# Centring two row pairs before PE turns them, with their layer-norm scale applied where values and key exponentials leave PSUM, and a new order of all steps

## The chip, the core and the metric

The kernel runs on one core of a Trainium2 chip. Five engines work beside each other, each with its own list of instructions: PE (matrix products and turns), ACT (activations, copies out of PSUM), DVE (vector work), POOL (elementwise work, memsets) and SP (which issues nearly all DMAs here). They meet through semaphores. The metric is the device time of one execution in microseconds. Before, it is 151.34 us (median of 3 runs, 151.34 to 151.38).

## What is computed

Rows x (2048 x 448) are layer-normalized to xn. The result is x plus a linear attention with a softmax feature map plus a dense layer with Mish, both on xn:

```python
xn = _layernorm(x, axis=-1)
return x + _A_ref(xn, A_wqkv, A_w_phi, A_wo) + _B_ref(xn, B_w1, B_b1, B_w2)
# _A_ref, 16 heads of 28:
pq = jnp.einsum("bhsd,hdf->bhsf", q, w_phi)
pk = jnp.einsum("bhsd,hdf->bhsf", k, w_phi)
phi_k = jnp.concatenate([_softmax(pk, axis=-1), _softmax(-pk, axis=-1)], axis=-1)
kv = jnp.einsum("bhsf,bhsd->bhfd", phi_k, v)
z  = jnp.einsum("bhsf->bhf", phi_k)
# phi_q likewise; num = phi_q kv, den = phi_q z + 1e-6, o = num / den, then o @ wo
# _B_ref: h = xn @ w1 + b1, act = Mish(h), act @ w2
```

The layer norm is (x - mean) / sqrt(var + 1e-5), without weights. So a row's scale, 1/sqrt(var + eps) (rstd), can be applied behind a product instead of ahead of it: (x - mean) W times rstd is xn W.

## The kernel before, in words

Tokens are handled as 16 tiles t of 128 rows, taken in 8 pairs u (tiles 2u and 2u+1). For each pair: statistics of both tiles (`ln_stats`: bn_stats and bn_aggr on DVE, or for one tile of the pair two passes with a sum on ACT), the scale (`ln_rstd` on ACT as Ln and Exp, or on POOL as a power), the normalized rows (`ln_pair` on DVE or POOL, three operations into one of four buffers xn), and the turn (`xT`: seven 128 x 128 blocks, by PE and copied out of PSUM into xnT, or as one DMA transpose from SP). A pair holds 7 blocks, since 448 = 3.5 x 128 and the two half blocks share one.

The turned rows feed the projections: `v_mm` (values), `k_mm` (keys, already through the feature map: the weights Wk and w_phi are multiplied once into Wpk, by `w_tr`, which turns Wk, and `w_mm`, which multiplies with the block-diagonal Wbd), `q_mm` (the same with Wpq) and `ffn1` (dense layer, W1). Such a projection holds two PSUM banks, one per tile, and is split into parts A, B (6 passes each) and H (2 passes); a pass is a matmul over 64 rows of the contraction, and two passes on the two halves of the array run side by side. All of it goes through the helper `run`, line 423. When the last part is done, ACT or DVE takes the banks out: keys and queries as Exp with both signs (L618 and L680), values as a copy (L510 or L512), the dense layer as Mish (L699). There are four pairs of banks, so at most four results are open.

Behind the keys, `k_norm` divides the exponentials by their sums (sums on DVE, the product on POOL, L630), `kv_mm` (L649) sums phi_k v over all rows, `kvz` turns that by a DMA, and `nd` (L722) gives numerators and denominators per tile; DVE divides, a DMA turns the result, `wo` (L845) and `ffn2` (L828) add up the output, DVE adds x (L793) and the rows are stored. The last tile is cut into 384 and 64 columns.

What sets the order is the string ORDER: it names every step, `run_order` calls them one after the other, and each call appends its instructions to the lists of the engines. Each engine works strictly in this order; semaphore waits come from the resources that a step reads and writes. A step's name carries kind, pair and engine: `xt2b` turns pair 2 by PE and copies it out on both ACT and DVE, `xt1m` turns pair 1 by DMA, `rs1a` is pair 1's scale on ACT, `wtk0b` and `wmk0b` are the turn and the product of the first half of Wk, `wmq0d` the query product with DVE copying out, `qd` the copy on DVE that doubles a part of WqT for that product, `lx1s` a load from SP (x2, x3, ... are row pairs; x4 and x6 load two pairs at once; `lkms` and `lvms` the main parts of Wk and Wv, `lkts` the last 64 rows of both, once per array half, called tails below; `lps` Wraw, that is w_phi; `l1ms`, `l1ts` the same of W1), `z12` twelve dummy matmuls of 512 columns on zeros (`warm`, L364), which keep PE working until the first data are there.

## Time and profile before

| what | value |
|---|---|
| time, median of 3 runs | 151.34 us |
| span of the profiled execution, first to last instruction | 148.7 us |
| that execution's own time around the span (151.34 - 148.7) | 2.6 us |
| ACT busy | 74.5 us (50%) |
| DVE busy | 102.4 us (69%) |
| POOL busy | 38.8 us (26%) |
| granted TensorE clock over the span | 1.000 |
| x loads of one pair, issue to landing | 3.0 us (4 loads of 224 KB) |

The page gives busy time per engine, a chain of work that ended last, and groups of instructions with their mean. The timeline gives rows in order of time: start, length, engine, line and operation, result and operands with shapes, count, and in brackets the idle time ahead of it with its releaser. A row with "x26" covers 26 instructions that follow one another. SPq rows are DMA issues; their landing is listed apart. Matmul lengths include the pipeline, so the pace is read from the starts or from a row's length over its count.

### The profile page before, as it was taken

The page shows a single profiled execution, that of the slowest core. Times are in us where ns is not written, and L with a number is a line of the kernel's source. Part 1 is how long each engine was busy: PE and PEld are TensorE (multiplying, and loading weights), DVE is VectorE, ACT ScalarE, POOL GpSimd, SP SyncE. Part 2 cuts the span into 40 slices and gives each one's busy share as a digit, 9 for nine tenths or more (in the row PEclk, how much of TensorE's full clock was granted, in tenths as well). Part 3 has the DMA queues.
Part 4 walks back from the last instruction along what each step waited for, and adds up shares of the span by engine and source line. Part 5 has one row for each costly group of instructions (what it writes and reads, how often), then busy time and mean ns, then how long its engine had stood idle before and what let it go on. Part 6 is the DMA issues. An engine that isn't in the chain of part 4 may idle for free.

```text
span 148.7 us, 3867 instructions
## 1 busy us (share of the span) xinstructions
PE 144.3 (97%) x1669; PEld 74.4 (50%) x1669; DVE 102.4 (69%) x229; ACT 74.5 (50%) x91; POOL 38.8 (26%) x53
## 2 busy tenths in 40 slices
PE   6999999999999999999999999999999999999993
PEld 2375555555544554444544445545555555555562
DVE  0599898996999940407697879539983999930072
ACT  3987999879999999657757762002000000000000
POOL 4423475079999993000000000000000000000000
PEclk9999999999999999999999999999999999999999
DMA  4998678799499159399856053120013040542005
GB/s 133 240 270 232 138 143 158 128 169 334 102 194 191 30 49 132 69 223 283 225 120 121 0 66 62 27 39 0 7 21 102 20 108 0 123 100 85 4 0 185
DMA packets 39964, 17.23 MB, mean 116 GB/s; under 512 B 33932, under 2 KB 39180, under 8 KB 39948
## 3 DMA queue, kind: packets, MB, share of 16 engines
q1 hardware_dynamic: 39776, 16.89, 53.4%
q8 instruction: 13, 0.21, 0.6%
q10 hardware_dynamic: 172, 0.10, 0.2%
q14 instruction: 3, 0.02, 0.0%
HBM read 7.02 MB, written 1.84 MB: 60 GB/s over the span
## 4 chain that ended last, share of the span: by engine, by line
PE 96%; DVE 1%; POOL 0%; issue 0%; POOLq 0%
PE PS L423 50%; PE PS L828 29%; PE PS L845 7%; PE PS L364 4%; PE PS L722 3%; PE PS L649 2%; PE PS L580 1%; DVE xn L497 1%; PE PS L505 1%; DVE x_all L793 0%; POOL v_all L339 0%; PE PS L556 0%; DVE x_all L814 0%; DVE b1T L512 0%; PE PS L693 0%
## 5 line engine op out<-in xcount | busy, mean ns | idle before, releaser
L423 PE MATMUL PS<-xnT,W 64*128 64x512 bf16 x392 | 44.8, 377 | 0.0
L828 PE MATMUL PS<-W,actT 128*128 128x448 bf16 (+1 forms) x224 | 42.9, 351 | 0.0
L699 ACT ACTIVATE actT<-PS,b1T 128x1024 bf16<-128x1024 f32 x28 | 29.8, 1112 | 22.1 <-PE PS L423 22.1
L828 PEld LDWEIGHTS PS<-W,actT 128*128 128x128 bf16 x224 | 21.5, 98 | 19.8 <-issue 0.3
L423 PEld LDWEIGHTS PS<-xnT,W 64*128 64x128 bf16 x392 | 18.0, 94 | 21.9 <-PE PS L423 1.9
L630 POOL TENSOR_TENSOR actT<-actT,rSk 128x896 bf16<-128x896 bf16 x16 | 26.6, 1699 | 5.1 <-DVE rSk L628 5.1
L793 DVE TENSOR_TENSOR x_all<-PS,x_all 128x448 bf16<-128x448 f32 (+1 forms) x16 | 9.2, 614 | 15.1 <-PE PS L845 10.5
L626 DVE TENSOR_REDUCE Sk<-actT 128x32 f32<-128x896 bf16 x16 | 16.6, 1037 | 1.1 <-ACT actT L618 1.1
L618 ACT ACTIVATE actT<-PS 128x896 bf16<-128x896 f32 x16 | 13.7, 920 | 1.8 <-PE PS L423 1.7
L423 PE MATMUL PS<-Wpk,xnT 64*128 64x448 bf16 x112 | 13.2, 349 | 0.0
L423 PE MATMUL PS<-Wkv,xnT 64*128 64x448 bf16 x112 | 12.9, 349 | 0.0
L423 PE MATMUL PS<-Wpq,xnT 64*128 64x448 bf16 x112 | 12.6, 349 | 0.0
L738 DVE COPY Sq<-PS 128x16 f32<-128x16 f32 x32 | 4.0, 167 | 12.0 <-PE PS L722 12.0
L462 DVE BATCH_NORM_STATS2 stats<-x_all 128x6 f32<-128x448 bf16 x14 | 8.4, 601 | 3.5 <-DMA x_all<-in_A_x_dram 3.5
L746 DVE TENSOR_TENSOR v_all<-v_all 128x464 f32<-128x464 f32 x16 | 10.3, 642 | 0.6
L742 DVE TENSOR_TENSOR v_all<-PS,Sq 128x464 f32<-128x464 f32 x16 | 10.3, 641 | 0.5
L749 DVE TENSOR_TENSOR xn<-v_all,rden 128x448 bf16<-128x448 f32 x16 | 10.0, 626 | 0.6
L744 DVE TENSOR_TENSOR v_all<-PS,Sq 128x464 f32<-128x464 f32 x16 | 10.1, 630 | 0.0
L680 ACT ACTIVATE actT<-PS 128x896 bf16<-128x896 f32 x10 | 8.6, 930 | 0.1
L423 PEld LDWEIGHTS PS<-Wpq,xnT 64*128 64x128 bf16 x112 | 5.4, 94 | 5.0 <-ACT actT L680 0.2
L423 PEld LDWEIGHTS PS<-Wkv,xnT 64*128 64x128 bf16 x112 | 5.4, 94 | 5.0 <-ACT actT L618 0.2
L423 PEld LDWEIGHTS PS<-Wpk,xnT 64*128 64x128 bf16 x112 | 5.4, 94 | 5.1 <-issue 0.2
(83 smaller groups left out, 119.3 us busy)
## 6 DMA issues: line engine op xcount, KB each, us to landing
W<-in_B_w_dram SPq DMA_DIRECT2D x1, 1568.0 KB, 9.3
...
W<-in_B_w_dram SPq DMA_DIRECT2D x1, 1344.0 KB, 6.5
...
```

Source lines behind the costliest of these rows:

```text
L423: ins = e.matmul(o, lhs(c, k), rhs(c, k), start=first and n == at[par][0], stop=last and n == at[par][-1])
L618: op("ACT", lambda e, s=s: e.activation(E_of(u)[:, s, :, :], two(b, D), ACT.Exp, scale=1.0 if s == 0 else -1.0), r=[pb(b), pb(b + 1)], w=[ ...
L626: op("DVE", lambda e: e.tensor_reduce(Sk[u][:, s, :], Eh(), AX.X, ALU.add), r=[("E", u, s)], w=[("Sk", u, s)], tag=f"Sk{u}.{s}")
L630: op("POOL", lambda e: e.tensor_tensor(Eh(), Eh(), ap_on(rSk[u][:, s, 0:1], [[1, 2 * H], [0, DH]]), ALU.mult), r=[("E", u, s), ("rSk", u, ...
L699: op("ACT", lambda e: e.activation(actT[:, fc, q * 1024:(q + 1) * 1024], bank(b, 2), ACT.Mish, bias=b1T[:, fc:fc + 1]), r=[("b1T",), pb(b) ...
L742: op("DVE", lambda e: e.tensor_tensor(tv(t1[i]), num(0), sx(1), ALU.mult), r=[pb(b), pb(b + 1), ("Sq", i, 1)], w=[("t1", i)], tag=f"ta{t}")
L744: op("DVE", lambda e: e.tensor_tensor(tv(t2), num(1), sx(0), ALU.mult), r=[pb(b), pb(b + 1), ("Sq", i, 0)], w=[("t2",)], tag=f"tb{t}")
L746: op("DVE", lambda e: e.tensor_tensor(t1[i], t1[i], t2, ALU.add), r=[("t1", i), ("t2",)], w=[("t1", i)], tag=f"tc{t}")
L749: op("DVE", lambda e: e.tensor_tensor(o_sb[(t // 2) % 2][:, t % 2, :].rearrange("p (h d) -> p h d", d=DH), t1[i][:, :, 0:DH], ap_on(rden[i ...
L793: op("DVE", lambda e: e.tensor_tensor(x_all[:, t, 0:n], bank(b)[:, 0:n], x_all[:, t, 0:n], ALU.add), r=[pb(b), ("x", t)], w=[("out", t)], ...
L828: ins = e.matmul(bank(b)[:, 0:width(t)], actT[:, fc, tok(t)], W2[:, fc, 0:width(t)], start=first and fc == 0, stop=last and fc == FC - 1)
L845: ins = e.matmul(bank(b)[:, 0:w], oT_of(u)[lo:hi, cc * P:(cc + 1) * P], Wo[lo:hi, cc, 0:w], start=first and n == at[par][0], stop=last and ...
```

## The change

Pairs 2 and 3 (CENT) are treated in two ways. For their values and keys the rows are only centred (`center`: x - mean, three operations on DVE), turned by PE (`xcT`) and copied into a free row of actT, not into xnT. The scale is applied at the exit: values leave PSUM tile by tile with scale rstd, and the exponentials of the keys as four activations of 448 columns with scale rstd or nrstd = -rstd (`neg_rstd`) in place of two of 896 with scale 1 or -1. For their queries and the dense layer, which need normalized rows in xnT, both pairs are normalized once more (`ln_pair` on POOL: xn3p, xn2p) and turned by DMA (xt3m, xt2m).

Statistics are now steps per tile (`st_dve`, `st_mean`, `st_var`), so that a mean can be had ahead of a variance. Both halves of Wk are turned into a pair of banks and copied out by ACT and DVE; of its last 64 rows only one copy is turned, and the copy out of PSUM doubles it. The tails of Wkv are loaded as keys and values together for one array half, values alone for the other. The dummy matmuls read a constant of ones that is there at the start, and there are eight. And ORDER is new throughout.

```diff
-pv table lx2s lba zero pm st2b lx3s lkms lps st3b lkts z12 pi b1 rs2p pw rs3a xn2d bd lx1s wtk0b lvms lx4s xn3d xt2b
-wtk1b wmk0b lqT2 xt3a v2Ha wmk1a v2Ba lqT0 st1 v3Ha lqT1 lqT3 rs1a v3Aa v2Aa st4 rs4p pk v3Ba k3H lx0s k3A qd xn1d
+lx3s lba pv lx2s pw sd6 table sm7 sm5 pi lkms lps z8 xc7 sv7 lt0s lvms lt1s pm xc6 bd lx1s sd4 lqT2 lx4s xc5 sv5 xc4
+b1 lqT1 ct3 wtk0b wtk1b ct2 rs2a sd3 sd2 sd9 wmk0a rs1a wmk1a rs3p nr2p xn3p lx6s xn1d sd8 sd11 v3Ha v2Hd v3Bd v2Ba
...
-                ins = e.matmul(bank(b)[:, :], ap_on(zeros[:, 0:1], [[0, P]]), ap_on(zeros[:, 0:1], [[0, TCW]]), start=True,
-                               stop=True)
+                ins = e.matmul(bank(b)[:, :], ap_on(ones, [[0, P]]), ap_on(ones, [[0, TCW]]), start=True, stop=True)
...
+    def load_kv_tail(eng, i):
+        (lo, hi), at = HALF[i], (0, D)[i]
+        dma(eng, lambda e: e.dma_start(Wkv[lo:hi, 3, at:2 * D], A_wqkv[384:448, D + at:3 * D]), w=[("Wt", i)],
+            tag=("ldWkv", "ldWvt")[i])
...
+    def center(t):
+        u = t // 2
+        for n, (lo, hi, at) in enumerate(parts_of_row(t)):
+            op("DVE", lambda e, lo=lo, hi=hi, at=at: e.tensor_scalar(
+                xn[u % NXN][:, at:at + hi - lo], x_all[:, t, lo:hi], mv[:, t, 0:1], None, op0=ALU.subtract),
+               r=[("x", t), ("mean", t)], w=[("xn", u % NXN, t % 2, n)], tag=f"xc{t}.{n}")
+
+    def neg_rstd(u, eng):
+        op(eng, lambda e: e.tensor_scalar(nrstd[:, 2 * u:2 * u + 2], rstd[:, 2 * u:2 * u + 2], -1.0, None, op0=ALU.mult),
+           r=[("rstd", u)], w=[("nrstd", u)], tag=f"nr{u}")
...
+    def xcT(u):
+        i = u % NXN
+        b = take2(False)
+        pe(lambda e: transpose7(e, b, xn[i], 3), [("xn", i, 0, 0), ("xn", i, 1, 0), ("xn", i, 1, 1), ("ident",)],
+           [pb(b), pb(b + 1)], f"xT{u}c")
+        for eng, lo, hi, bb, n in (("ACT", 0, 3, b, 0), ("DVE", 3, 7, b + 1, 1)):
+            at = (u % 2) * 7 * P
+            evac(eng, lambda lo=lo, hi=hi: actT[:, CROW, at + lo * P:at + hi * P],
+                 lambda lo=lo, hi=hi, bb=bb: bank16(bb)[:, 0:(hi - lo) * P], [pb(bb)], [("xcT", u, n)],
+                 f"xT{'hf'[n]}{u}c")
...
+    def scaled(eng, dst, src, t, r, w, tag):
+        if eng == "ACT":
+            op("ACT", lambda e: e.activation(dst(), src(), ACT.Copy, scale=rstd[:, t:t + 1]), r=r, w=w, tag=tag)
+        else:
+            op("DVE", lambda e: e.tensor_scalar(dst(), src(), rstd[:, t:t + 1], None, op0=ALU.mult), r=r, w=w, tag=tag)
...
     def k_mm(u, part):
         def then(b):
+            if u in CENT:
+                for s in range(2):
+                    for i in range(2):
+                        op("ACT", lambda e, s=s, i=i: e.activation(
+                            E_of(u)[:, s, i, :], bank(b + i)[:, 0:D], ACT.Exp,
+                            scale=(rstd, nrstd)[s][:, 2 * u + i:2 * u + i + 1]),
+                           r=[pb(b + i), ("rstd", u), ("nrstd", u)], w=[("E", u, s)] if i else [("Eh", u, s)],
+                           tag=f"exkc{u}.{s}{i}")
+                return
```

What the new order moves is shown at three places. The first is PE's start, from the dummies on. L364, L693, L556, L505, L580 and L423 are the dummies, the turn of the bias b1, the turns of Wk, the turns of rows, the products with Wbd and the projections' passes. Before:

```order
L364 MATMUL PS<-zeros 128x512 x12
L693 MATMUL PS<-ident,b_rows 128x14
L556 MATMUL PS<-ident,Wkv 112x128 x8
L505 MATMUL PS<-ident,xn 128x128 x7
L556 MATMUL PS<-ident,Wkv 112x128 x8
L580 MATMUL PS<-Wbd,Eq 128x112 x8
L505 MATMUL PS<-ident,xn 128x128 x7
L423 MATMUL PS<-Wkv,xnT 128x448 x2
L580 MATMUL PS<-Wbd,Eq 128x112 x8
L423 MATMUL PS<-Wkv,xnT 128x448 x26
L423 MATMUL PS<-Wpk,xnT 128x448 x8
L580 MATMUL PS<-Wbd,WqT 128x112 x16
```

The same place now (the lines are those of the changed kernel):

```order
L376 MATMUL PS<-const-bfloat16-1.0 128x512 x8
L759 MATMUL PS<-ident,b_rows 128x14
L529 MATMUL PS<-ident,xn 128x128 x7
L590 MATMUL PS<-ident,Wkv 112x128 x12
L590 MATMUL PS<-ident,Wkv 112x64 x4
L529 MATMUL PS<-ident,xn 128x128 x7
L614 MATMUL PS<-Wbd,Eq 128x112 x16
L434 MATMUL PS<-Wkv,actT 128x448 x28
L434 MATMUL PS<-Wpk,actT 128x448 x22
L614 MATMUL PS<-Wbd,WqT 128x112 x16
```

A turn of rows stands first now, both halves of Wk follow one another, the two products with Wbd too, and no value pass stands ahead of them; 22 key passes in place of 8 stand ahead of the query product.

The second place is ACT, from the scale of the first pairs to the first values. Before:

```order
L510 ACTIVATE Eq<-PS 112x512 [waits done_PE]
L510 ACTIVATE xnT<-PS 128x384 [waits done_PE]
L510 ACTIVATE Eq<-PS 112x512 [waits done_PE]
L510 ACTIVATE Wpk<-PS 128x448 [waits done_PE]
L510 ACTIVATE xnT<-PS 128x896 [waits done_PE]
L510 ACTIVATE Wpk<-PS 128x896 [waits done_PE,done_DVE]
L476 ACTIVATE lnv<-mv,eps_col 128x2 [waits done_DVE]
L478 ACTIVATE rstd<-lnv 128x2 [waits done_ACT]
L510 ACTIVATE v_all<-PS 128x32x28 [waits done_PE] x2
```

There now (Eq is the buffer that holds the turned Wk, lnv and rstd are the scale):

```order
L534 ACTIVATE actT<-PS 128x384 [waits done_PE]
L534 ACTIVATE Eq<-PS 112x512 [waits done_PE] x2
L534 ACTIVATE actT<-PS 128x384 [waits done_PE]
L487 ACTIVATE lnv<-mv,eps_col 128x2 [waits done_ACT]
L489 ACTIVATE rstd<-lnv 128x2 [waits done_ACT]
L534 ACTIVATE Wpk<-PS 128x896 [waits done_PE,done_DVE]
L487 ACTIVATE lnv<-mv,eps_col 128x2 [waits done_DVE]
L489 ACTIVATE rstd<-lnv 128x2 [waits done_ACT]
L534 ACTIVATE Wpk<-PS 128x896 [waits done_PE]
```

Pair 1's scale, which waits for DVE's statistics of pair 1, stood behind the second copy of Wpk; now it stands ahead of it.

The third place is SP's queue, from the last turns of WqT on. L517 (now L541) are the DMA turns of rows, L688 (L754) those of query exponentials, L278 (L285) the tails of W1. Before:

```order
L270 DMA x_all<-in_A_x_dram 128x896
L270 DMA x_all<-in_A_x_dram 128x1792
L517 DMA_TRANSPOSE xnT<-xn 128x7x128 [waits done_DVE]
L278 DMA W<-in_B_w_dram 64x1792 x2
L517 DMA_TRANSPOSE xnT<-xn 128x7x128 [waits done_DVE]
L517 DMA_TRANSPOSE xnT<-xn 128x7x128 [waits done_POOL]
L688 DMA_TRANSPOSE EqT<-Eq 128x8x128 [waits done_ACT]
```

There now:

```order
L541 DMA_TRANSPOSE xnT<-xn 128x7x128 [waits done_DVE]
L541 DMA_TRANSPOSE xnT<-xn 128x7x128 [waits done_POOL]
L277 DMA x_all<-in_A_x_dram 128x896
L285 DMA W<-in_B_w_dram 64x1792 x2
L541 DMA_TRANSPOSE xnT<-xn 128x7x128 [waits done_POOL]
L541 DMA_TRANSPOSE xnT<-xn 128x7x128 [waits done_DVE]
L280 DMA W<-in_B_w_dram 128x3x1792
L541 DMA_TRANSPOSE xnT<-xn 128x7x128 [waits done_POOL]
```

These are the turns of pairs 1 and 3, a load of x and the tails of W1, then pairs 4 and 6, W1's main part, and pair 5. Before, pairs 1, 4 and 5 were the first three turns by DMA, and W1's main part was loaded behind all of them. Further on, all query projections stand ahead of the dense layer's first passes, where before three of them stood among those, and the KV products, which were spread over three places, stand together ahead of the sixth group of the dense layer.

More of the change, by code (lines that the diff above doesn't have):

```diff
@@ L227, in _kernel, with xcT_of @@
     FE = FC - NU
+    CENT = (2, 3)
+    CROW = 3
+    def xcT_of(u, c):
+        return actT[:, CROW, (u % 2) * 7 * P + c * P:(u % 2) * 7 * P + (c + 1) * P]
     def E_of(u):
@@ L311, in table @@
            tag="table")
-    def p_zero():
-        op("POOL", lambda e: e.memset(zeros[:], 0.0), w=[("zeros",)], tag="zeros")
     def p_ident():
@@ L445, in step, with st_dve, st_mean, st_var @@
         return add
[L449 to L465 removed]
+    def st_dve(t):
+        op("DVE", lambda e: e.bn_stats(stats[:, t, :], x_all[:, t, :]), r=[("x", t)], w=[("st", t)], tag=f"bn{t}")
+        op("DVE", lambda e: e.bn_aggr(mv[:, t, :], stats[:, t, :]), r=[("st", t)], w=[("mv", t), ("mean", t)],
+           tag=f"ag{t}")
+    def st_mean(t):
+        i = t // 2 % 2
+        op("ACT", lambda e: e.activation(junk[i][:], x_all[:, t, :], ACT.Copy, scale=1.0 / D, accum_out=mv[:, t, 0:1]),
+           r=[("x", t), ("junk", i)], w=[("mean", t), ("junk", i)], tag=f"sm{t}")
+    def st_var(t):
+        i = t // 2 % 2
+        op("ACT", lambda e: e.mul(rmean[:, i:i + 1], mv[:, t, 0:1], D ** -0.5), r=[("mean", t)], w=[("rmean", i)],
+           tag=f"rm{t}")
+        op("ACT", lambda e: e.activation(junk[i][:], x_all[:, t, :], ACT.Square, bias=rmean[:, i:i + 1],
+                                         scale=-D ** -0.5, accum_out=mv[:, t, 1:2]),
+           r=[("x", t), ("rmean", i), ("junk", i)], w=[("mv", t), ("junk", i)], tag=f"sq{t}")
     def ln_rstd(u, eng):
@@ L620, in then @@
                    r=[pb(b), pb(b + 1)], w=[("E", u, s)], tag=f"exk{u}.{s}")
-        pair_part(f"k{u}", part, tok_works(u, Wp[1]), [("xnT", u), ("xnU", u)] + [("Wp", 1, h, c) for h in range(2) for c in range(2)], then)
+        pair_part(f"k{u}", part, works_of(u, Wp[1]), turned(u) + [("Wp", 1, h, c) for h in range(2) for c in range(2)], then)
     def k_norm(u, s):
@@ L701, in then @@
                r=[("b1T",), pb(b), pb(b + 1)],
-               w=[("act", fc, q)] + ([("E", fc - FE, s) for s in range(2)] if fc >= FE else
+               w=[("act", fc, q)] + [("xcT", u, n) for u in CENT for n in range(2) if fc == CROW] + ([("E", fc - FE, s) for s in range(2)] if fc >= FE else
                                      [x for i in range(3) if EQ_ROWS[i] == fc for x in (("Eq", i, 0), ("Eq", i, 1), ("Eqp", i))]), tag=f"mish{q}_{fc}")
@@ L867, in _kernel @@
     for u in range(NU):
-        add(f"st{u}", ln_stats, u)
-        add(f"st{u}b", ln_stats, u, True)
+        for t in (2 * u, 2 * u + 1):
+            add(f"sd{t}", st_dve, t)
+            add(f"sm{t}", st_mean, t)
+            add(f"sv{t}", st_var, t)
+            add(f"xc{t}", center, t)
+        for eng, c in (("DVE", "d"), ("POOL", "p")):
+            add(f"nr{u}{c}", neg_rstd, u, eng)
+        add(f"ct{u}", xcT, u)
         add(f"xt{u}b", xT, u, "both")
@@ L911, in _kernel @@
             add(f"l{n}m{c}", load_main, eng, "W" + n, t, A_wqkv[:, (i + 1) * D:(i + 2) * D])
-        add(f"lkt{c}", load_tail, eng, "Wkv", Wkv, A_wqkv[:, D:3 * D])
+        for i in range(2):
+            add(f"lt{i}{c}", load_kv_tail, eng, i)
         add(f"l1m{c}", load_main, eng, "W1", W1, B_w1)
@@ L921, in _kernel @@
     add("qd", double_qT)
-    for n, fn in (("pi", p_ident), ("pm", p_mask), ("pw", p_wbd), ("pv", p_ones), ("pk", p_kvt), ("pp", p_pads), ("zero", p_zero)):
+    for n, fn in (("pi", p_ident), ("pm", p_mask), ("pw", p_wbd), ("pv", p_ones), ("pk", p_kvt), ("pp", p_pads)):
         add(n, fn)
-    for n in (1, 2, 4, 8, 12):
+    for n in (6, 8, 10, 12):
         add(f"z{n}", warm, n)
```

109 lines of the change are left out of this document (55 added, 54 removed).

## Prediction

> **What bounds the kernel now.** I read the page's busy table first, then the chain of work that ended last, then the timeline of the first 16 us.
>
> ```profile
> PE 144.3 (97%) x1669; PEld 74.4 (50%) x1669; DVE 102.4 (69%) x229; ACT 74.5 (50%) x91; POOL 38.8 (26%) x53
> ```
>
> PE is busy almost all of the time. Busy is not the same as useful, so the chain in order of time (start, length, what) comes next.
>
> ```profile
> 1.39 5.30 PE PS L364 x12
> ...
> 10.72 3.32 PE PS L423 x34
> 14.04 0.89 PE PS L580 x16
> 14.94 36.24 PE PS L423 x370
> 51.18 0.88 PE PS L649 x96
> ...
> 59.45 7.90 PE PS L423 x72
> ...
> 143.25 2.42 PE PS L828 x14
> ```
>
> The first 5.30 us are twelve dummy matmuls. From 10.7 us on, PE runs one pass of the projections (L423, 448 columns, two half-arrays side by side) every 3.32/34 = 0.098 us, and 36.24/370 = 0.098 us over the next 36 us. It holds this pace without a gap, and only the last addition and store follow 145.7 us. So the kernel is "time at which PE becomes dense" plus a fixed amount of PE work plus a tail. A change can win only ahead of 10.7 us, and every wait of PE behind that point is lost in full.
>
> What holds PE back ahead of 10.7 us is in the timeline (start, length, engine, line, operation).
>
> ```profile
> 3.54 0.58 ACT L453 ACTIVATE junk<-x_all 128x448 bf16<-128x448 bf16 x1 [1.46 <-DMA x_all<-in_A_x_dram]
> 4.02 0.19 ACT L453 ACTIVATION_READ_ACCUMULATOR junk<-x_all 128x1 f32 x1
> ...
> 6.63 0.19 ACT L458 ACTIVATION_READ_ACCUMULATOR junk<-x_all,rmean 128x1 f32 x1
> ...
> 6.94 1.13 DVE L497 TENSOR_SCALAR xn<-x_all,mv,rstd 128x448 bf16<-128x448 bf16 x3
> 6.99 0.82 PE L556 MATMUL PS<-ident,Wkv 128*112 128x128 bf16 x8 [0.18 <-DMA Wkv<-in_A_wqkv_dram]
> 7.32 1.16 POOL L539 TENSOR_TENSOR Wbd<-Wraw,mask 112x224 bf16<-112x224 bf16 x2 [0.52 <-DMA Wraw<-in_A_w_phi_dram]
> 7.84 0.60 ACT L510 ACTIVATE Eq<-PS 112x512 bf16<-112x512 bf16 x1 [0.46 <-PE PS L556]
> 8.32 0.88 DVE L497 TENSOR_SCALAR xn<-x_all,mv,rstd 128x448 bf16<-128x448 bf16 x3
> 8.53 0.61 PE L556 MATMUL PS<-ident,Wkv 128*112 128x128 bf16 x8
> 8.73 0.49 ACT L510 ACTIVATE xnT<-PS 128x384 bf16<-128x384 bf16 x1 [0.29 <-PE PS L505]
> ...
> 9.86 0.36 PE L423 MATMUL PS<-Wkv,xnT 64*128 64x448 bf16 x2
> 10.65 2.63 PE L423 MATMUL PS<-Wkv,xnT 64*128 64x448 bf16 x26
> ```
>
> The row statistics (on ACT from 3.54 to 6.63 + 0.19 = 6.82), then the scales and the normalized rows (DVE, 6.94 and 8.32), run ahead of PE's turns of pairs 2 and 3. Two other chains run beside them and depend on no row of x: the key weights land at 6.99 and are turned and copied out; the feature matrix Wraw lands at 7.3 and POOL builds Wbd until 7.32 + 1.16 = 8.48. At 10.65 all set-up is done and 26 of the first 28 value passes are left, so before is as if it became dense at 10.65 - 2 x 0.098 = 10.45.
>
> **Term 1: the start.** In the new order the first turn (pair 3, centred) needs the means alone: x lands at 3.54, the mean is there at 4.02 + 0.19 = 4.2, and three centring operations take about 0.9 (row 8.32), so its operands stand at 5.3. That chain is off the path. What is left:
> - Wbd, as before, at 8.48. The first product (8 matmuls, 0.45, since 16 take 0.89 in the chain) runs from 8.5 to 8.95.
> - ACT ends its statistics at 6.8 as before, copies half a turned pair (0.49, row 8.73), then Wk's first half (from 7.84, 0.60), then the second half. That one needs the first tail of Wkv, then 0.4 of PE, so ACT has it from about 8.4 to 9.0, and pair 2's half to 9.45.
> - The second product runs 9.0 to 9.45, and the value passes follow.
>
> The tail and the value weights are read from the issues and their landings.
>
> ```profile
> L278 SPq DMA_DIRECT2D Wkv<-in_A_wqkv_dram x1: 561/561/561, 2.7 to 2.7; - x1
> ...
> DMA to landing us min/median/max: 5.0/5.0/5.0
> L273 SPq DMA_DIRECT2D Wkv<-in_A_wqkv_dram x1: 434/434/434, 4.6 to 4.6; - x1
> ...
> DMA to landing us min/median/max: 4.9/4.9/4.9
> L270 SPq DMA_DIRECT2D x_all<-in_A_x_dram x1: 585/585/585, 4.0 to 4.0; - x1
> ...
> DMA to landing us min/median/max: 4.6/4.6/4.6
> L270 SPq DMA_DIRECT2D x_all<-in_A_x_dram x1: 486/486/486, 5.1 to 5.1; - x1
> ...
> DMA to landing us min/median/max: 5.6/5.6/5.6
> ```
>
> The first tail lands at 7.7, the value weights at 9.5, rows of pair 1 at 8.6, pairs 4 and 5 at 10.7. From 7.7 to 9.5 a tail (112 KB), 224 KB and 336 KB arrive, 370 KB per us. In the new order the value weights (336 KB) and a tail of 56 KB come straight behind the first tail: 7.7 + 392/370 = 8.75, not later than 9.5. So PE is dense at 9.45 (bounds 9.4, from Wbd alone, and 9.8, with the weights at their old time and a copy late). **Gain 1.0 us**, bounds 0.65 and 1.05. Most of it is not the missing scale: it is that nothing of the rows stands between the weight products any more.
>
> **Term 2: new waits behind the start.** Three places have little slack.
>
> ```profile
> 10.32 0.61 DVE L462 BATCH_NORM_STATS2 stats<-x_all 128x6 f32<-128x448 bf16 x1
> ...
> 11.06 0.59 DVE L462 BATCH_NORM_STATS2 stats<-x_all 128x6 f32<-128x448 bf16 x1
> ...
> 10.89 0.93 ACT L510 ACTIVATE Wpk<-PS 128x896 bf16<-128x896 f32 x1
> 11.91 0.30 ACT L476 ACTIVATE lnv<-mv,eps_col 128x2 f32<-128x2 f32 x1
> 12.24 0.20 ACT L478 ACTIVATE rstd<-lnv 128x2 f32<-128x2 f32 x1
> ```
>
> (a) The second copy of Wpk stands behind pair 1's scale on ACT. Pair 1 now lands behind the value weights: 8.75 + 224/370 = 9.35. Two statistics at 0.74 each (10.32 to 11.06) end at 10.85, the scale (11.91 to 12.44) at 11.4, the copy (0.93) at 12.3. The key passes need it at 9.45 + 28 x 0.098 = 12.2. Loss 0.1; without x's delay nothing, with x 0.4 later 0.5.
>
> (b) The query product needs the doubled query weights, a copy on DVE behind pair 4's first statistics (x at about 10.9), three normalizing operations (0.88) and two more statistics: 10.9 + 0.74 + 0.1 + 0.88 + 1.48 + 0.1 + 0.23 = 14.4. PE is there at 12.3 + 22 x 0.098 = 14.45. Loss 0.1, bounds 0 and 0.4 (a large x load later by as much).
>
> ```profile
> L517 SPq DMA_TRANSPOSE xnT<-xn x6: 1222/1234/1627, 14.4 to 27.4; - x6
> ...
> DMA to landing us min/median/max: 2.9/3.1/4.5
> W<-in_B_w_dram SPq DMA_DIRECT2D x1, 1344.0 KB, 6.5
> ```
>
> (c) On SP, pair 4's turn now follows pair 1's, pair 3's, a load of x (224 KB) and two tails of W1 (2 x 224 KB). Pair 1's rows stand at 12.6; the issues take 1.63 (the first turn's, the longest), 1.23 (the median), 0.5 and 2 x 0.6 (the L270 and L278 rows), 4.6 together, so pair 4's turn is issued at 17.2 and lands 3.1 later, and 0.6 more behind the added 224 KB: 20.9. PE comes there after the query product (0.89) and 56 passes: 14.55 + 0.89 + 5.47 = 20.9. Loss 0.25, bounds 0 and 0.7. **Sum of the waits 0.45**, bounds 0 and 1.6.
>
> **What should cost nothing.**
>
> ```profile
> 14.97 0.98 ACT L510 ACTIVATE Wpq<-PS 128x448 bf16<-128x448 f32 x2 [0.49 <-PE PS L580]
> 15.84 3.43 ACT L618 ACTIVATE actT<-PS 128x896 bf16<-128x896 f32 x4
> 32.01 24.88 POOL L630 TENSOR_TENSOR actT<-actT,rSk 128x896 bf16<-128x896 bf16 x15 [0.76 <-DVE rSk L628]
> L699 ACT ACT_TABLE_LOAD x2 | 2.6, 1283 | 0.0
> ```
>
> The scales on the way out of PSUM split ACT's operations: per key pair four of 0.49 for two of 0.86, per value pair two of 0.49 for one of 0.86. That is 0.24 and 0.12 per pair, 0.7 in all; the trace has no ACT copy with a scale per row, and I take the plain copy's 0.49 (bounds 0.43, half a wide one, and 0.58, the statistics pass at 3.54). Two more scales on ACT cost 1.05. Against that, all query pairs now come ahead of the first Mish, so one table load of the page's line is left of three, 2.6 us less. ACT needs some 34 us for keys, queries and values, PE 336 x 0.098 = 32.9, and four bank pairs let PE run up to about 5 us ahead. That hides it; with ACT 2 us slower than this, the excess would be PE's. POOL gets two more pairs to normalize and starts its 16 products of 24.88/15 = 1.66 near 24 us: with one scale and one memset it ends at 52. PE asks for the last one behind the 20.9 + 0.25 of (c), 230 more passes (22.5), 76 passes of the dense layer at 7.90/72 = 0.11 (8.4) and seven of eight KV products at 0.88/3 = 0.29 (2.0): at 54. The KV products are pulled forward, so of this cover 2 us are left. The extra x turns on the DMA queue lie under passes, except (c).
>
> **Sum.** The profiled execution spans 148.7, and 151.34 - 148.7 = 2.6 lies around it. 148.7 - 1.0 + 0.45 = 148.15, so **150.8 us** against the median of 151.34.
>
> **Rivals.**
>
> *PE stays at half rate* (slower). The dummies take 5.30/12 = 0.44 for 512 columns; the last L828 group, the output tile that is cut to 384 columns, takes 2.42/14 = 0.173. That is twice the rate, and the dummies never reach it in 5.3 us of unbroken work; the first turns at 6.99 (8 in 0.82) are slower than those at 8.53 (8 in 0.61). The new kernel has eight dummies, 3.5 us, over at about 4.4, then scattered turns with idle time until 7. If PE must earn the full rate anew from 7.0 by the same 5.3 us, it gets it at 12.3. The set-up after 7.0 is about 2.1 us of PE at full rate, 4.2 at half, so the values start at 11.2 in place of 9.45, and 1.1 us of passes at half pace lose 0.55 more: 2.3. The waits (a) to (c) then vanish behind it: 151.34 - 1.0 + 2.3 = 152.6. It decides if the change of rate comes after about 10.5. For it: 12 dummies were not enough by themselves. Against: nothing shows that scattered turns don't count, and a start 0.5 us earlier (the new dummies need no memset) helps.
>
> The Trainium skill, "TensorE: Matmul & The Clock Gate", Part 1, says that PE runs at half its clock until it was busy through one free-running window of about 3.4 us. The trace agrees with the half rate (0.44 against 0.173 x 512/384 = 0.23), but shows more than 5.3 us. By that rule eight dummies fill a window only if one happens to begin near the first of them; otherwise the time would be near this rival's.
>
> *The waits take it all.* (a) to (c) at their upper ends, or W1's main load (1344 KB, 6.5 us to landing), now ahead of pair 5's turn, which PE needs near 28 us: 1.0 to 1.6 back, 151.3 to 151.9, middle 151.5. For it: three arrivals within 0.3 us of their need. Against: all three were estimated from a queue that has idle stretches.
>
> *The waits come to nothing.* 151.34 - 1.0 = 150.35, or 150.3 at the bound of 1.05.
>
> **How the numbers follow.** Forecast 0.45 (own range 150.5 to 151.1), no waits 0.15, waits take it all 0.18, half rate 0.22. About 0.2%, 0.3 us, is what a measurement of this kernel can tell from no change. Faster by more: 0.42 of the forecast, 0.15, and 0.02 of the third, 0.59. Within: 0.03 of the forecast, 0.10 of the third, 0.03 of a mild half rate, 0.16. Slower: 0.06 and 0.19, 0.25. The range, 150.2 to 152.5, leaves out the worse half of the half rate and the best of the bounds.
>
> **What would show it.** Value passes (source Wkv) starting at 9.4 to 9.8 in the timeline, with 0.098 us per pass from the first, prove term 1 and refute the half rate; 0.19 per pass there would confirm it. Gaps of PE in front of the first Wpk passes (released by ACT), of the Wpq product (by DVE) and of pair 4's value passes (by a DMA) give (a), (b), (c). A PE gap ahead of the KV products would mean that POOL was late, gaps released by ACT between 20 and 45 us that the split exponentials cost more than their cover. Were PE dense from 9.45 on and the time still not less, the tail would have grown, which I don't expect.

## The result and the profile after

The changed kernel takes **162.06 us** (median of 4 runs, 161.79 to 163.3) against 151.36 of the kernel before on the same chip: a ratio of **1.072** (95% 1.068 to 1.077), 7% slower. Forecast were 150.8 and at most 152.5. The profiled execution, the longest of the four (163.3 us), spans 161.5 us, 12.8 more than before.

The page of the changed kernel: engines with busy time, the granted clock in 40 slices, and the shares of the chain that ended last.

```profile
PE 152.5 (94%) x1665; PEld 73.8 (46%) x1665; DVE 104.7 (65%) x230; ACT 74.6 (46%) x99; POOL 42.6 (26%) x58
...
PEclk9999999999999999699999999999999999999999
...
PE 87%; DMA 5%; ACT 2%; issue 2%; SPq 0%; DVE 0%; ACTq 0%
```

PE is still the engine that is busy nearly always, and 8 us busier although it issues four matmuls fewer: its pieces became longer. The chain in order of time says where (start, length, what):

```profile
11.04 2.60 PE PS L434 x12
13.68 1.90 PE PS L434 x18
...
19.11 0.95 PE PS L434 x8
20.10 1.33 PE PS L434 x12
21.48 1.33 PE PS L434 x12
22.85 2.46 PE PS L434 x24
...
30.78 1.73 ACT actT L684 x2
32.56 3.48 DMA xnT<-xn
...
58.95 2.11 PE PS L715 x243
61.06 2.02 issue
63.34 5.26 PE PS L434 x32
```

Where before has one piece of 370 passes in 36.24 us, there are now pieces of 8 to 28 passes. Three things are to be seen. The first 12 passes take 2.60/12 = 0.22 each, not 0.098. From 19 us on the chain breaks after every few passes though no other engine is named: 12 passes need 1.18 and have 1.33 + 0.05 (21.48 to 22.85 is 1.37). And inside the KV products (L715) PE stands for 2.02 us, after which 32 dense passes take 5.26 (0.164 each, 0.11 before). A fourth, pair 2's late turn at 32.56, will matter below.

The start, from the timeline of PE:

```profile
0.85 3.57 PE L376 MATMUL PS<-const-bfloat16-1.0 128*128 128x512 bf16 x8 [0.85 <-PEq L1037]
4.35 0.19 PE L759 MATMUL PS<-ident,b_rows 14*128 14x14 bf16 x1
5.02 0.93 PE L529 MATMUL PS<-ident,xn 128*128 128x128 bf16 x7 [0.48 <-DVE xn L518]
6.64 2.04 PE L590 MATMUL PS<-ident,Wkv 128*112 128x128 bf16 x16 [0.69 <-DMA Wkv<-in_A_wqkv_dram]
8.61 0.93 PE L529 MATMUL PS<-ident,xn 128*128 128x128 bf16 x7
9.33 1.70 PE L614 MATMUL PS<-Wbd,Eq 112*128 112x112 bf16 x16
10.97 2.64 PE L434 MATMUL PS<-Wkv,actT 64*128 64x448 bf16 x16
```

The products with Wbd take 1.70 for 16 matmuls (0.56 for 8 before), seven turns 0.93 (0.56 before): PE works at half rate until 12.8 in this execution. The values begin at 10.97, not 9.45.

For the chain's breaks, the group of weight loads (PEld) of the dense layer's passes, before and after; behind the bar stand busy time, mean ns, then the idle time ahead and what released it.

```profile
L423 PEld LDWEIGHTS PS<-xnT,W 64*128 64x128 bf16 x392 | 18.0, 94 | 21.9 <-PE PS L423 1.9 <-issue 0.6
```

```profile
L434 PEld LDWEIGHTS PS<-xnT,W 64*128 64x128 bf16 x392 | 17.2, 96 | 26.5 <-PE PS L434 9.5 <-issue 1.3 <-DVE KVT L726 0.3
```

Idle time released by PE itself rose from 1.9 to 9.5 us in this group alone. One such place in the changed kernel's timeline of PEld:

```profile
19.10 0.49 PEld L434 LDWEIGHTS PS<-Wpk,xnT 64*128 64x128 bf16 x8 [0.67 <-ACT actT L677]
20.10 0.30 PEld L434 LDWEIGHTS PS<-Wpk,xnT 64*128 64x128 bf16 x6 [0.50 <-PE PS L434]
...
21.47 0.11 PEld L434 LDWEIGHTS PS<-Wkv,xnT 64*128 64x128 bf16 x4 [0.50 <-PE PS L434]
```

The reason is in `pe_pass`: part B of a projection works on the same two banks as A and H, with the halves of the array exchanged, and so waits until the part of the other kind is done.

```python
o = pe(fn, r, [pb(b), pb(b + 1)], tag, after=[side[b, "A" if part == "B" else "B"]] if part in "ABH" and
       (b, "A" if part == "B" else "B") in side else [])
```

Before has 65 such waits, and in none of them the awaited part stands directly ahead. The new order has 74, and in **31 the awaited part is the one just issued** (`v2Ba lqT3 v2Aa`, `f1.3A f1.3B`). From one matmul's start to the next these 31 take 0.41 to 0.44 us, against 0.19 to 0.215 elsewhere: 0.23 each, 31 x 0.23 = 7.1. I call them direct neighbours.

The KV products end so (PE's timeline):

```profile
58.88 2.18 PE L715 MATMUL PS<-actT,v_all 128*30 128x56 bf16 x244
63.08 0.26 PE L715 MATMUL PS<-actT,v_all 128*30 128x56 bf16 x12 [2.02 <-issue]
```

POOL had ended its last product at 58.3, so nothing that they read was late. A packet of 16 KB of instructions (queue q8 of the page) starts at 60.73, and PE stands from 60.86 to 63.08. The granted clock is at half from 64.15 to 67.56.

To compare the kernels I add up, from the starts of the matmuls, by how much each operation of PE exceeds its usual length (0.567 for a part A of a key projection, 0.648 in the dense layer, and so on), by stretch of time:

| kernel | first value pass | excess to 30 us | 30 to 50 | 50 to 70 | 70 to 107 | last matmul starts |
|---|---|---|---|---|---|---|
| before | 9.86 | 0.28 | 0.03 | 0.66 | 0.40 | 145.99 |
| changed | 10.97 | 3.40 | 2.60 | 5.27 | 2.15 | 158.78 |
| sep2kv | 9.82 | 2.43 | 4.03 | 2.97 | 0.73 | 154.06 |
| mixnew | 11.38 | 2.30 | 2.08 | 1.28 | 0.39 | 151.52 |
| finG | 9.64 | 2.62 | 0.50 | 1.05 | 0.37 | 148.48 |

(The last three are experiments.) So the loss is spread over everything ahead of 107 us; it isn't one place.

### The profile page after: what moved, and what is told of

It reads as the page before. It is cut to its first block, busy times and chain, and to the rows that moved or that the text cites. A ratio compares the mean times of both kernels' runs of the same rounds, so it can differ in the third digit from the quotient of the medians.

```text
span 161.5 us, 3876 instructions
## 1 busy us (share of the span) xinstructions
PE 152.5 (94%) x1665; PEld 73.8 (46%) x1665; DVE 104.7 (65%) x230; ACT 74.6 (46%) x99; POOL 42.6 (26%) x58
## 4 chain that ended last, share of the span: by engine, by line
PE 87%; DMA 5%; ACT 2%; issue 2%; SPq 0%; DVE 0%; ACTq 0%
PE PS L434 48%; PE PS L894 26%; PE PS L911 7%; DMA Wkv<-in_A_wqkv_dram 3%; PE PS L788 2%; DMA xnT<-xn 2%; PE PS L715 1%; ACT actT L677 1%; PE PS L590 1%; ACT actT L684 1%; PE PS L614 1%; PE PS L529 1%; SPq L277 0%; DVE x_all L859 0%; DVE x_all L880 0%
## 5 line engine op out<-in xcount | busy, mean ns | idle before, releaser
L434 PE MATMUL PS<-xnT,W 64*128 64x512 bf16 x392 | 49.0, 387 | 0.9
L434 PEld LDWEIGHTS PS<-xnT,W 64*128 64x128 bf16 x392 | 17.2, 96 | 26.5 <-PE PS L434 9.5
L859 DVE TENSOR_TENSOR x_all<-PS,x_all 128x448 bf16<-128x448 f32 (+1 forms) x16 | 9.7, 618 | 28.1 <-PE PS L894 28.1
L434 PE MATMUL PS<-Wpq,xnT 64*128 64x448 bf16 x112 | 13.4, 350 | 0.6 <-DMA xnT<-xn 0.2
L434 PE MATMUL PS<-Wpk,xnT 64*128 64x448 bf16 x84 | 10.6, 351 | 0.6 <-ACT actT L677 0.2
L684 ACT ACTIVATE actT<-PS 128x896 bf16<-128x896 f32 x12 | 10.4, 918 | 1.1 <-PE PS L434 1.0
L434 PE MATMUL PS<-Wkv,xnT 64*128 64x448 bf16 x84 | 10.6, 350 | 0.1
L746 ACT ACTIVATE actT<-PS 128x896 bf16<-128x896 f32 x10 | 8.6, 914 | 2.3 <-PE PS L434 2.1
L502 POOL TENSOR_SCALAR xn<-x_all,rstd,shift 128x448 bf16<-128x448 bf16 (+2 forms) x12 | 7.1, 610 | 6.2 <-DVE shift L496 4.8
L434 PEld LDWEIGHTS PS<-Wpq,xnT 64*128 64x128 bf16 x112 | 5.1, 94 | 7.6 <-PE PS L434 3.0
L507 DVE TENSOR_SCALAR xn<-x_all,mv,rstd 128x448 bf16<-128x448 bf16 (+2 forms) x12 | 6.9, 629 | 1.0 <-ACT rstd L489 1.0
```

Of the source, the lines that this page charges most:

```text
L434: ins = e.matmul(o, lhs(c, k), rhs(c, k), start=first and n == at[par][0], stop=last and n == at[par][-1])
L684: op("ACT", lambda e, s=s: e.activation(E_of(u)[:, s, :, :], two(b, D), ACT.Exp, scale=1.0 if s == 0 else -1.0), r=[pb(b), pb(b + 1)], w=[ ...
L859: op("DVE", lambda e: e.tensor_tensor(x_all[:, t, 0:n], bank(b)[:, 0:n], x_all[:, t, 0:n], ALU.add), r=[pb(b), ("x", t)], w=[("out", t)], ...
```

## The experiments

Ratios are to the kernel before on the same chip, with a 95% interval. In kernels other than the changed one lines may be numbered one lower (L433 for L434); those made from the kernel before keep its lines (L423). In diffs, a line is a piece of ORDER.

**Three suspects, one by one and together.** Parts of other projections put between direct neighbours (sep), the KV products in groups (kv3), twelve dummies (z12), all three (all3).

```diff
 sep
-v3Ha v2Hd v3Bd v2Ba lqT3 v2Aa nr3d v3Aa rs4p k3B lqT0
+v3Ha v2Hd v3Bd v2Ba lqT3 k3B v2Aa nr3d v3Aa rs4p lqT0
...
 kv3
-f1.1B f0.8A e14 f1.0H f1.0B f1.0A kv2 kv6 kv3 kv5 kv0 kv1 e0 kn7.0 kv4 kv7
+f1.1B kv6 kv1 kv5 f0.8A e14 f1.0H f1.0B kv4 kv0 f1.0A e0 kn7.0 kv3 kv2 kv7
...
 z12
-lps z8 xc7
+lps z12 xc7
```

> The changed kernel with only the order of projection parts altered: wherever part A or H of a projection stood directly behind part B of the same projection (or the other way round), another projection's part is put between; 31 such places become none. Theory 1 (each direct neighbour makes PE wait for its own last pass, 0.23 us a place): 31 x 0.23 = 7.1 us less, 155 us. Theory 2 (PE is late because ACT's split exits and the DMA turns are late, and the waits on itself only fill that time): under 2 us less, 160 to 162 us, with PE's gaps moved to places released by ACT or DMA.

> The changed kernel with only the eight KV products spread over three places (3, 2 and 3 of them) with dense-layer parts between. Theory 1 (512 short PE instructions in a row run ahead of their supply: PE stops 2.2 us inside the last KV product, then works 3.4 us at half clock, which costs 1.7): 3.9 us less, 158.2 us, no drop of the granted clock between 60 and 80 us. Rival (PE stopped there for POOL's last normalized keys): the stop stays in front of the last KV product, same time within 0.5 us.

> The changed kernel with twelve dummy matmuls in place of eight. Half-rate theory (eight dummies do not bring PE to full rate, so set-up and the first twelve or so value passes run at half pace): value passes at 0.098 us from the first, 1.0 to 1.6 us less, 160.5 to 161 us, and a smaller spread between runs than 1.5 us. Rival (the first passes are slow because their operands come late): the same time within 0.3 us, or 0.3 more for the longer dummies.

> The changed kernel with all three edits: parts separated, KV products in three places, twelve dummies. Theory 1, causes add: 162.1 - 7.1 - 3.9 - 1.3 = 149.8 us, within 1 us. Theory 2 (late exits and turns bound PE once the waits are gone): 154 us or more.

Measured: sep **163.34** (1.080, 1.076 to 1.083), kv3 160.53 (1.061, 1.057 to 1.064), z12 161.53 (1.065, 1.059 to 1.071), all3 161.51 (1.070, 1.066 to 1.075). Theory 1 as I had put it falls: with no direct neighbour left the time rose. The waits of PE in sep, summed by who released them (us in total, times, longest):

```profile
PE PS L433 <- DMA xnT<-xn: 2.8, 1, 2.8
...
PE PS L433 <- ACT actT L764: 1.3, 4, 0.4
...
PE PS L433 <- ACT Wpk L533: 0.9, 1, 0.9
...
PE PS L433 <- DVE KVT L725: 0.8, 1, 0.8
PE PS L433 <- ACT actT L676: 0.8, 1, 0.8
```

My edit had pulled parts forward that open a projection (k3B above), and these came to banks that ACT hadn't emptied; and PE, sooner at pair 2's queries, stood for their turn. The self-waits were gone and others of the same size were there; behind the longest of them the granted clock was at half for 3.4 us (35.85 to 39.27), some 1.7 us more. all3, in which no direct neighbour is left either, is no faster than kv3 alone.

kv3 has no stretch at half clock behind the KV products, as theory 1 had it, but the stop stayed. It stands in the last of the three groups, 1.6 us from one start to the next, and the time fell by some 1.5 us in place of 3.9:

```profile
PE PS L714 <- issue: 1.4, 1, 1.4
```

z12 brought the first value pass to 9.24 at full pace, 1.7 us earlier, and the time fell by 0.5 only, less than the intervals can tell. In its profiled execution the wait for pair 2's turn grew from 0.4 to 1.9, the stop in the KV products was 2.9, and PE stood for the query weights, which it had not done in the changed kernel. The copy that doubles them (L297, on DVE) waited for the last of their loads:

```profile
15.62 0.23 DVE L297 COPY WqT<-WqT 128x256 bf16<-128x256 bf16 x1 [1.60 <-DMA WqT<-in_A_wqkv_dram]
```

```profile
15.91 0.96 PE L613 MATMUL PS<-Wbd,WqT 112*128 112x112 bf16 x16 [1.23 <-DVE WqT L297]
```

**The price of a direct neighbour by itself**, in the kernel before, in a stretch where ACT has slack:

```diff
 pairs14
-f1.0A f1.1H f1.13B f1.0H f1.13H f1.0B
+f1.0A f0.5B f1.13H f1.13B f1.0H f1.0B
...
```

> Edit: the kernel before, with 14 pairs of its passes of the dense layer exchanged so that 14 parts B stand directly beside part A or H of their own projection; nothing else moves. The cost of one such place by itself: theory 1, 14 x 0.23 = 3.2 us on top of 151.1, 154.3, each of the 14 gaps 0.41 to 0.44 us long. Rival (it is only seen where PE would wait for ACT anyway): 151.1 to 151.4.

154.73 (1.024, 1.021 to 1.026): 3.51 us for 14 places, **0.25 each**. Its PEld group shows the same signature as the changed kernel's:

```profile
L423 PEld LDWEIGHTS PS<-xnT,W 64*128 64x128 bf16 x392 | 17.1, 94 | 26.0 <-PE PS L423 8.5 <-issue 0.4
```

So theory 1's price is right where nothing else is late, and the rival (only seen where PE waits anyway) is refuted for that stretch.

**Neighbours apart without opening earlier**, alone and with the KV groups; and the changed order without centring.

```diff
 sep2 (in sep2kv, made from kv3, other parts stand between)
-f1.11H f1.11B f1.6H f1.6A f0.2H f0.2B f1.6B
+f1.6B f1.11H f1.6A f1.11B f0.2B f1.6H
...
 nocent
-CENT = (2, 3)
+CENT = ()
-z8 xc7 sv7 lt0s lvms lt1s pm xc6 bd
+z8 sv7 lt0s lvms lt1s pm rs3a xn3d bd
...
```

> Edit: in the changed kernel all 31 places where a part B stands directly beside part A or H of its own projection are taken apart again, this time so that no part that opens a projection comes to PE before ACT has emptied its bank pair (the first attempt did that and lost 9 us there). Centring, scaled exits, the KV burst and the eight dummies stay. Theory 1 (the direct neighbours cost 31 x 0.23 = 7.1 us, and the first attempt only failed by its new bank waits): some 6.4 net, 162.1 - 6.4 = 155.7 (155 to 156.5). Theory 2 (the new order is short of free banks or of DMA turns, and PE waits as long in any order of its parts): 160.5 or more.

> Edit: the same for the changed kernel with its KV products in three groups (160.5 us before this edit); 2 of 29 direct neighbours stay. Theory 1: 160.5 less about 5.2 net = 155.3 (154.5 to 156). Theory 2: 159.5 or more.

> Edit: the changed kernel's order with no pair centred: pairs 2 and 3 are normalized by DVE as before, no scale at the exits, no second turn of their rows. The order of all other work, with its 31 direct neighbours and its KV burst, stays. Theory 1 (the new order is what costs the time, not the centring): 162 plus 0.5 to 2 for a later start of the values, 162.5 to 164, with 31 gaps of 0.41 to 0.44. Rival (the scaled exits on ACT and the second turns cost it): back to 151 to 155.

sep2 162.14 (1.067, 1.059 to 1.075; runs from 159.97 to 163.42), sep2kv 158.76 (1.049, 1.047 to 1.052), nocent 165.24 (1.093, 1.089 to 1.097). The last is clear: **without centring the new order is 3 us slower still** (1.2 above theory 1's range), the values beginning at 12.42. It isn't the centring that costs the 11 us. sep2 met theory 2's number. Its profile has two stretches at half clock (7.25 to 14.07 and 61.86 to 68.69), the second twice as long as the changed kernel's, and two stops in the KV products of 3.6 us in all in place of one of 2.0; these take part of what the neighbours had cost. In sep2kv (between its two theories), where that didn't happen in the second place, PE's waits read

```profile
PE PS L433 <- DMA xnT<-xn: 3.1, 3, 1.2
PE PS L714 <- issue: 1.5, 1, 1.5
...
PE PS L433 <- ACT actT L683: 0.7, 2, 0.4
```

and SP's timeline shows why turns of x (L540) are late:

```profile
21.68 0.59 SPq L279 DMA_DIRECT2D W<-in_B_w_dram  x1
22.32 1.24 SPq L540 DMA_TRANSPOSE xnT<-xn  x1
23.60 6.79 SPq L753 DMA_TRANSPOSE EqT<-actT  x2
30.43 2.15 SPq L753 DMA_TRANSPOSE EqT<-Eq  x1
32.63 2.66 SPq L540 DMA_TRANSPOSE xnT<-xn  x2
```

W1's main load of 1344 KB is issued at 21.68, in the new order ahead of pair 5's turn. It lands at 29.3, two turns of query exponentials behind it take 6.79 us to issue, and pair 2's turn, for which its rows stood ready at 25.7, goes out at 32.63.

**Those transfers moved**, alone (turns) and with the parts once more rearranged (turns2).

```diff
 turns, SP's steps alone
-xt1m xt3m l1ts xt4m xt6m l1ms xt5m e2 e3 e7 xt2m xt0m e6 e8 xt7m e9
+xt1m xt3m l1ts xt4m xt6m xt5m xt2m e2 e3 e7 xt0m e6 e8 xt7m l1ms e9
```

> Edit: the kernel of sep2kv (parts apart, KV in three groups, 158.8 us), with two issues of SP moved and nothing else: W1's main load (1344 KB) behind the last turn of x, where the kernel before has it, and pair 2's second turn ahead of the turns of pair 1's query exponentials. In sep2kv PE waits 4.4 us between 17 and 42 us for turns of x that queue behind these. Theory A (the turns behind W1's load are what the early passes wait for, and nothing else is): 4 us of these gaps go, 158.8 - 4.0 = 154.8 (154.3 to 155.3). Theory B (ACT is next: from 17 to 50 us the new order asks it for two exponentials of 0.81 per 1.32 us of passes, some 4 us more than PE's own time): the gaps released by SP go, and 3 to 4 us released by ACT take their place, 157.5 to 159.

> Edit: turns, with the parts of the projections put in another order that has no direct neighbour left and the fewest waits that I could find. Theory A: 153.5. Theory B (ACT's exponentials bound that stretch in any order of the passes): gaps released by ACT of 4 to 5 us in all between 17 and 56 us, 155.5 to 157.

161.18 (1.064, 1.057 to 1.070) and 160.89 (1.061, 1.056 to 1.067): slower than sep2kv, against both theories' numbers. The turns of x did come in time, and the wait went 10 us on. In turns, from the timelines of SP, ACT and PE:

```profile
39.92 5.88 SPq L753 DMA_TRANSPOSE EqT<-Eq  x1
```

```profile
48.56 1.73 ACT L745 ACTIVATE actT<-PS 128x896 bf16<-128x896 f32 x2 [4.19 <-PE PS L433]
```

```profile
50.34 3.85 PE L433 MATMUL PS<-xnT,W 64*128 64x512 bf16 x18 [2.63 <-ACT actT L745]
```

W1's load now blocks SP from 38 on (one turn took 5.88 to issue), PE stands until 50.34 for a bank that ACT empties late, and the clock falls to half from 50.64 to 54.05. In turns2 there are gaps released by ACT, 3.5 us in six places (theory B expected 4 to 5; the lines show five of them, 3.1 us), and 0.6 released by DVE:

```profile
PE PS L433 <- ACT actT L676: 1.0, 1, 1.0
...
PE PS L433 <- ACT actT L745: 0.8, 1, 0.8
PE PS L433 <- ACT Eq L745: 0.8, 2, 0.4
PE PS L433 <- DVE v_all L535: 0.6, 1, 0.6
...
PE PS L433 <- ACT actT L683: 0.5, 1, 0.5
```

I read this as PE, ACT and SP's queue being within a few us of each other from 15 to 55 us in this order: in these runs what was taken from one was found at the next. Before is different there: 19 parts of the dense layer, which ask ACT for one Mish of about 1.1 per 1.5 us of passes, stand ahead of the last keys and queries, which ask it for two exponentials of 0.81 per 1.32. In the new order one dense part does.

**The KV burst**, in the kernel before with five products together (kv5), later in mixnew with all eight (burst8).

```diff
 kv5
-f0.13B kv7 kv4 e10 kv6 f0.13H f0.6H f0.6A kn3.0 f0.10A f0.6B kn1.1 f0.10B kv3 kv1
+f0.13A e10 f0.13H f0.6H f0.6A kn3.0 f0.10A f0.6B kn1.1 f0.10B kv7 kv4 kv6 kv3 kv1
...
 burst8
-f0.0A kv0 f0.0H f1.0B kn7.1 e15 f1.4B f1.0H f1.0A kv3 f0.4H e1 kv7
+f0.0A f0.0H f1.0B kn7.1 e15 f1.4B f1.0H f1.0A f0.4H e1 kv2 kv4 kv5 kv6 kv1 kv0 kv3 kv7
...
```

> Edit: the kernel before, with its second group of KV products (7, 4, 6) moved to the third (3, 1), so that five stand together, and one exchange of two parts so that no direct neighbour arises; nothing of the change is in it. Theory 1 (PE's instructions, 64 per product of 0.26 us, are used up faster than they are fetched): PE stops 1.5 to 2.2 us inside the fourth or fifth product, as in kv3 and in the changed kernel, and with about 0.8 of new waits for ACT the time is 151.2 + 2.3 to 3 = 153.5 to 154.2. Rival (the stop comes from something else that the new order brings, a DMA or POOL): no stop inside a product, 151.2 + 0.8 = 152.0.

> Edit: mixnew with its eight KV products put together where the last one stands; four more direct neighbours arise. The burst by itself: theory 1 (512 instructions in 2.1 us outrun the fetching of PE's instructions): one stop of 1.5 to 2.3 us inside one of the last products, and some 1.7 more in runs in which the granted clock then falls to half for 3.4 us; with 4 x 0.23 = 0.9 for the neighbours mixnew + 2.5 to 5. Rival (the burst is harmless, and the stop was due to what surrounds it): mixnew + 0.9.

kv5 (its product 7 reads exponentials that a Mish has overwritten by then; the work is the same): 152.1 (1.004, 1.002 to 1.007), no stop, the rival's number. burst8: 157.51 (1.039, 1.037 to 1.041), 1.8 more than mixnew, between the rival's 0.9 and theory 1's 2.5 at least, with

```profile
PE PS L714 <- issue: 2.0, 1, 2.0
```

in the eighth product, as in the changed kernel, and the clock at full this time. So five together are harmless in that place, eight are not. Their number isn't the whole condition: kv3 has a stop with groups of three, two and three (54.7 to 61.4), and finE below has one of 1.1 us in a product that stands alone, 0.9 us behind four others. The instruction packets say more: in before they start at 50.10, 53.93 and 59.04, 3.8 to 5.1 us apart, each after 246 to 335 more instructions of PE; in the changed kernel at 56.13 and 60.73, and in between PE used 495 and then had none. In no run do two packets start less than 3.3 us apart, and in every run with such a stop it ends 2.1 to 3.1 us after a packet has started. That PE waits for its own instructions there is read from these times; I didn't change the fetching itself, so it isn't shown.

**The same operations in other orders.** mixnew is written from the changed order, mixold from the order before; all operations of the change are in both.

```diff
 mixnew, the KV products
-f1.0H f1.0B f1.0A kv2 kv6 kv3 kv5 kv0 kv1 e0 kn7.0 kv4 kv7
+f1.1A kv2 f1.1B f1.3H kv4 kv5 kn3.0 f1.3B kn0.1 f0.3B kv6 f0.3H kn7.0 f0.3A f0.0B kv1
...
 finG, SP's steps alone
-xt1m xt3m l1ts xt4m xt6m l1ms xt5m e2 e3 e7 xt2m xt0m e6 e8 xt7m
+xt1m xt3m xt4m xt2m xt5m xt0m l1ts xt6m xt7m l1ms e3 e2 e7 e6
...
```

> Edit: the changed kernel's operations, all of them (centring, scaled exits, second turns), in another order: 4 direct neighbours in place of 31, the KV products in ones and twos over 8 us, turns of x ahead of those of the query exponentials, and keys, queries and values so mixed that ACT is not asked for more than it can do. Still all queries ahead of the dense layer. Theory 1 (the listed order of the changed kernel costs the 11 us, by self-waits, the KV burst, and queues of SP and ACT that take turns, and the centring itself costs nothing): the time of before or a little over, 151.2 to 153. Rival (centring with its second turns and split exits has a price of its own that no order hides): 155 or more.

> Edit: the same operations in an order derived from that of the kernel before: 19 parts of the dense layer stand ahead of the last projection of keys and queries, W1's main load behind the early turns of x, 2 direct neighbours, KV products in small groups; pairs 2 and 3 are centred, and their queries come behind the first keys. Theory 1: 150.9 to 152.5. Rival (a price of the centring): 155 or more.

mixnew 155.7 (1.028, 1.025 to 1.031) and mixold 156.93 (1.036, 1.033 to 1.038). Both meet the rival's number (155 or more). But more than 5 us of the loss went away by order alone, and most of what was left lay ahead of 50 us, with a late and slow start in both (11.38 and 12.53). In mixnew a load of x had come ahead of the weights. So three more, with twelve dummies and the loads of the start as in the changed kernel; then a last one.

> Edit: all operations of the change (centring, scaled exits, second turns; twelve dummies), in an order derived from that of the kernel before: parts of the dense layer among the last queries, KV products in small groups, W1's main load behind the early turns, one direct neighbour, the first loads in the changed kernel's order. Theory 1 (only the order costs; the centring brings the values some 0.6 us earlier than in before, 9.24 against 9.86 as in the run with twelve dummies): 150.4 to 151.6, so at most 0.5 percent faster than before. Rival (a price of the centring of 2 us or more that no order hides, as mixnew and mixold could still be read): 153 or more.

> Edit: as finF, a second order found in the same way (two direct neighbours). Theory 1: 150.4 to 151.6. Rival: 153 or more.

> Edit: mixnew with twelve dummies and with the loads of the start in the changed kernel's order (in mixnew a load of x stood ahead of the weights and the values began at 11.4 us, at half rate until 14.5); all queries stay ahead of the dense layer, 3 direct neighbours. Theory 1: the values begin at 9.3 at full rate, 155.7 - 2.1 - 1.0 = 152.6, and up to 0.5 less by fewer waits. Rival: an earlier start only meets later turns and exponentials, 154.5 to 155.7.

> Edit: finF's operations once more, with no direct neighbour, with the eight KV products never more than three within 4 us, and with PE's other waits of finF (0.99 for ACT near 43 us) removed by order; the product of the query weights still waits for their last turned load near 16 us, where PE has nothing else (finF lost 2.3 us there). Theory 1 (only the order costs; what the centring gains at the start, 0.6 us, is given back at that wait for the query weights): 153.5 less 1.0 for the KV stop and 1.0 for the wait for ACT = 151.5 (151 to 152.2), about the time of before. Rival (something else in the centred kernel costs 2 us): 153 or more.

finF 153.52 (1.015, 1.011 to 1.020), finE 154.59 (1.025, 1.020 to 1.029), finB 159.91 (1.052, 1.046 to 1.058), **finG 153.23** (1.012, 1.009 to 1.015). finB missed its number by 7 us and its rival's by 4: PE, starting early, stood 3.5 us for the query weights (until 18.12) and 2.1 us for a bank that DVE emptied late (until 35.92); these come from its longest execution, 163.32. All of finF, finE and finG lie where their rival had them, at 153 or more. finG did what was asked of the two waits (no stop at the KV products, the wait of 0.99 for ACT gone), yet came to 153.23 and not 151.5. Its row at 16 us:

```profile
16.06 0.96 PE L613 MATMUL PS<-Wbd,WqT 112*128 112x112 bf16 x16 [1.14 <-DVE WqT L297]
```

PE has used up all passes for which something is turned, and waits for the query weights (1.3 in the starts), then 0.3 and 0.7 for turns of pairs 1 and 6. These 2.3 us are of the size of what keeps it above before; no run takes them away, so that they are its cause isn't shown. None of my orders beat the kernel before.

## Why the prediction was wrong

**The sum missed its largest term.** The step that failed is "plus a fixed amount of PE work": for PE behind the start I had three waits, (a) to (c), 0.45 us and at most 1.6, and put all else at nothing without reading the new order for it. The table has 13.4 us of excess there in the changed kernel against 1.4 in before, 12 us more. I costed what the change adds to ACT, POOL and SP, and of PE only the start. The parts' places on PE in the new order I didn't read, past the first passes, for who waits for whom. The sentence "It holds this pace without a gap" was true of before, where no part B stood beside its own A or H; the change put 31 there. A price of 0.25 each is shown alone by pairs14; in the changed order the gaps are 0.23 longer each.

**"Every wait of PE behind that point is lost in full" is half right.** It holds where only PE is late (pairs14). Between 15 and 55 us of the new order it doesn't: sep took away some 6.5 us of waits and got none back, since ACT's banks and SP's turns were the next to be late. So the changed kernel's own loss can't be split into terms that add up, and what each of its causes costs stays open.

**Term 1, the gain of 1.0.** The data are there as I worked out: with PE at full rate the values begin at 9.24 (z12). But in the profiled execution, with eight dummies, PE runs at half rate until 12.8, and they begin at 10.97. That is the first rival (11.2, and 1.1 us of passes at half pace; it was 10.97 and 1.8). It had 0.22, and its time of 152.6 was 9 us short of the rest. Which of the two comes is a matter of the execution: sep and kv3, with the same eight dummies and the same start, were at full rate from 5.1 and 5.2 on, and their values began at 9.14 and 9.58.

**Term 2.** (a) and (b) came to nothing in the changed kernel, (c) too, all behind the late start; with the early one of kv3 (c) is a wait of 0.8 at 23 us, above its bound of 0.7. With early starts (b) is the larger miss: PE waits 1.2 us for the query weights in z12 and 1.0 to 3.5 in finE, finG, finF and finB, where I had 0.1 and at most 0.4. The working of (b) counted DVE's operations ahead of the copy and left out the last load that the copy needs, which is what it waits for in z12 (and by its own numbers, 14.4 against 14.45, it gave no loss). The turn that did hurt was pair 2's, behind W1's main load and three turns of exponentials: 0.4 us in the changed kernel, 1.9 in z12, 2.8 in sep. I had named that load in the second rival, for pair 5, and called the queue one with idle stretches.

**"What should cost nothing".** POOL ended at 58.3 and PE came to the products at 58.9, so POOL's cover held, though both were later than worked out (52 and 54) and PE's delay helped. But the products pulled together have a cost of their own, which I looked for on POOL only: a stop of 2.2 us and, in that execution, 3.4 us at half clock, 1.7 more. The times don't show the latter: the execution of 162.2 us had a mean granted clock of 1.000 and those of 161.79 and 161.93 one of 0.989. ACT's split exits are small as such (0.52 from one start to the next for 448 columns, 0.81 for 896, so 0.23 a pair of operations, as worked out). But the claim that ACT's 34 us are covered by PE's 32.9 gave ACT no room, and in turns2 most of PE's waits between 16 and 54 us are released by it once the turns are on time.

**What the centring itself does.** With the centring taken out, the new order is 3 us slower (nocent), in part by a start of the values that is 1.4 us later. Put into better orders, the change stays 1.2% above before (finG): its first passes need less, but the queries of pairs 2 and 3 need second turns, and PE runs out of turned rows near 16 us. Whether an order exists that hides these 2 us, or whether they are a price of the centring as the rivals of mixnew and finG had it, stays open. Of the 10.7 us about 9 went away by another order and four more dummies, with all operations of the change kept (162.06 to 153.23).
